# A scheduler that lets instruction packets arrive later, and later still behind queued transfers: the same instructions in another order

## The chip, the cores and the metric

The kernel runs on one core of a Trainium2 chip. The metric is device time in microseconds (us) of one execution; lower is better. Of the core's engines this text names PE (matrix products; its weight loads are a row of their own, PEld), DVE and ACT (elementwise work), POOL, and SP, which here only starts DMA transfers.

## The reference

The input `x` has shape (8, 3200, 256). A filter in the frequency domain comes first, then a gated convolution of what it returns. Cut to what matters:

```python
X = np.fft.rfft(x, axis=1)
Yr = X.real @ w_r - X.imag @ w_i + b_r
Yi = X.real @ w_i + X.imag @ w_r + b_i
Yr, Yi = shrink(Yr), shrink(Yi)          # sign(v) * max(|v| - 0.01, 0)
y = np.fft.irfft(Yr + 1j * Yi, n=3200, axis=1)

gate = sigmoid(sum(conv_w[k] * y_padded[:, k:k + 3200, :] for k in range(5)))
out = (gate * (y @ w_val)) @ w_out
```

## The kernel before, in words

The Fourier transform of length 3200 is split as 64 x 50. Each of the 8 batches goes through two halves.

*Into frequencies.* Eight pieces per batch load `x` and multiply by a 50-point matrix (PE, line 582, tile `p`; line 548 for the first batch). ACT copies the result to `s`, and SP stores it to `a_dram`. From there it comes back transposed as `a`. Thirteen units per batch then do the 64-point step (line 633, `s`), the mixing with `w_r` and `w_i` as three products (line 708 into `k_bank`, line 703 into `y_ps`, lines 666 and 667 for the last unit), bias and threshold on DVE and ACT (`yb`, `tp`), and, for two units at a time, the inverse 64-point step (line 746, `z_ps`; line 738 for the last unit). ACT copies that to `z_t`, SP stores it to `z_dram`.

*Out of frequencies and through the gate.* Eight blocks per batch load `zl` from `z_dram`, which needs the whole batch there, and do the inverse 50-point step (line 802, `y_p`). One `y_p` group is 32 products in the program. The trace shows each product in full fp32 as two weight loads and two matmuls, so the group is 64 weight loads and 64 matmuls of 50 columns. ACT copies it into `y_sb`; ACT and DVE run the five taps and the sigmoid into `acc` (lines 856, 859, 870). PE forms `v_ps` from `y_hl`, DVE multiplies it with the gate (line 901), PE forms `o_ps` from `gated`, and ACT and SP bring `out` home (lines 925 and 927).

*What sets the order.* Nothing here is run in the order in which it is written. `Plan` collects pieces of work with an engine, a duration, their inputs and a due time `at`, and `Plan.order` plays them through on a model of the core. At each step it takes, of the engine that can start first, the piece with the smallest due time among those that can start within some 20 ns. The order so found is the order in which the instructions are issued; on the chip each engine then follows its list strictly and waits on semaphores. The dictionary `O` holds offsets of the due times, one per kind of piece, some for one batch alone, and five other numbers that weigh the choice. They decide the order and nothing else: the pieces, their instructions and their buffers stay the same.

The model also has a rule for PE's instructions. It takes it that PE starts with room for `AHEAD` of them, that a packet of `PACKET` more is asked for each time another `PACKET` have run (the first time after `TRIGGER`), and that a packet can be used `FETCH` ns after it was asked for. A piece of PE whose instructions are not there yet is late in the model, and another may be taken ahead of it. The model's count, `ins`, has matmuls and weight loads in it, not the instructions that only wait on a semaphore. `lines` and `pipe` are the model's times by which the transfers issued so far are done.

Of the kernel before, what the change touches and what calls it, by code (L numbers as in the profile page):

```python
# [83 lines left out]
class Plan:  # L84
# [11 lines left out]
    def add(self, at, engine, busy, fn, uses=(), sets=(), new=None, delay=None, mode="r", kb=0, chain=None, extra=0, moves=1, ways=16, ins=0):  # L96
        n = len(self.pieces)
        before = set()
        for key in uses:
            before |= set(self.writers.get(key, ()))  # L100
        for key in sets:
            before |= set(self.readers.get(key, ())) | set(self.writers.get(key, ()))
        for key in uses:
            self.readers.setdefault(key, []).append(n)
        for key in sets:
            self.writers[key], self.readers[key] = [n], []
        p = dict(n=n, at=round(at, 5), engine=engine, busy=busy, fn=fn, before=before, new=new or {}, mode=mode, kb=kb, extra=extra, moves=moves, ways=ways, ins=ins,
                 tiles={key[:2] for key in (*uses, *sets)}, delay=busy + LAND[engine] if delay is None else delay)
        p["behind"] = {self.last[chain]} if chain in self.last else set()
        if chain:  # L110
            self.last[chain] = n
        self.pieces.append(p)
        return n

    def order(self):
# [25 lines left out]
        mode, pipe = "r", 0.0  # L141
        lines = {10: 0.0, 13: 0.0, 16: 0.0}
        landings = [0.0] * LANES
        ran, fetched = 0, []
        done = []

        def opens(p):
            at = 0.0
            for tag in p["new"].values():
                row = rows[tag]  # L150
                if len(row) >= self.slots[tag]:
                    old = row[len(row) - self.slots[tag]]
                    if users[old]:
                        return None
                    at = max(at, ends[old])
            return at

        while len(done) < len(pieces):
            best = None
            for e in engines:  # L160
                could = []
                for p in waiting[e]:
                    at = opens(p)
                    if at is not None:
                        if p["ins"] and ran + p["ins"] > AHEAD:
                            k = (ran + p["ins"] - AHEAD + PACKET - 1) // PACKET
                            at = max(at, fetched[k - 1] - p["busy"] * max(0, AHEAD + PACKET * (k - 1) - ran) / p["ins"])
                        could.append((max(free[e], p["ready"], at, landings[-LANES] if p["kb"] else 0.0,
                                           max(lines[10], pipe) - BACKLOG if p["kb"] and p["at"] > FIRST else 0.0), p))
                if not could:  # L170
                    continue
                first = min(c[0] for c in could)
                near = [c for c in could if c[0] <= first + SLACK[e]]

                lone = e == "PE" and sum(c[1]["mode"] == "q" for c in near) < O["crowd"]
                if e == "PE" and mode == "q":
                    stay = max(SLACK[e], 100 * min(O["stay"], 4.0))
                    near = [c for c in could if c[0] <= first + (stay if c[1]["mode"] == "q" else SLACK[e])]
                start, p = min(near, key=lambda c: (c[1]["at"] + (0.0 if e != "PE" or c[1]["mode"] != "q" else -O["together"] if mode == "q"
                                                                   else O["hold"] if lone else 0.0), c[0]))  # L180
                if best is None or start < best[0]:
                    best = start, p
            assert best is not None, "no piece can begin"
            start, p = best
            e = p["engine"]
            waiting[e].remove(p)
            busy, delay = p["busy"], p["delay"]
            if e == "PE":
                slow = max([f for until, f in CLOCK if start < until], default=1.0)
                busy, delay = busy * slow, delay * slow  # L190
                to = SWITCH.get(mode + p["mode"], 0)
                busy, delay, mode = busy + to, delay + to, p["mode"]
                while PACKET * len(fetched) + TRIGGER <= ran + p["ins"]:
                    fetched.append(start + p["busy"] * (PACKET * len(fetched) + TRIGGER - ran) / p["ins"] + FETCH)
                ran += p["ins"]
            if p["kb"]:
                ways = p["ways"]
                for n in lines:
                    if n <= ways:
                        lines[n] = max(lines[n], start + LEAD) + p["kb"] * 1024 / ways / RATE  # L200
                pipe = max(pipe, start + LEAD) + p["kb"] * 1024 / PIPE[ways]
                delay = max(pipe, *(lines[n] for n in lines if n <= ways)) + TAIL - start + p["extra"]
                landings += [start + delay] * p["moves"]
            free[e] = start + busy
            end = start + delay
            p["start"], p["end"] = start, end
            done.append(p)
            for t, tag in p["new"].items():
                rows[tag].append(t)
            for t in p["tiles"]:  # L210
                if t in users:
                    users[t] -= 1
                    ends[t] = max(ends[t], end)
            for n, at in [(n, end) for n in after[p["n"]]] + [(n, start) for n in follow[p["n"]]]:
                q = pieces[n]
                q["left"] -= 1
                if q["engine"] == "PE" != e and at == end:
                    at += WEIGHTS
                q["ready"] = max(q["ready"], at)
                if not q["left"]:  # L220
                    waiting[q["engine"]].append(q)
# [15 lines left out]
LEAD, RATE, TAIL = 1080, 20.2, 1270  # L237
PIPE = {10: 235, 13: 300, 16: 324}
LANES = 8
AHEAD, PACKET, TRIGGER, FETCH = 449, 256, 130, 5000  # L240
BACKLOG = 5000
FIRST = -27

# [5 lines left out]
def act(n, kind="copy"):  # L249
# [3 lines left out]

NU = (NT + 1) // 2
T = float(NU)
O = {'stay': -18.479,
     'crowd': -190.568,
     'hold': -218.696,
     'together': 48.138,
     'later': 144.105,  # L260
     'load_x': 172.107,
     'p1': -0.768,
     'p1_step': 1.776,
     'load_a': -165.726,
     's2': -1.563,
     's1i': 3.16,
     'p3': -2.062,
     'load_z': -222.529,
     'y': 23.715,
     'conv': 23.753,  # L270
     'val': 7.511,
     'gate': 9.461,
     'project': 10.677,
     'late_val': 7.079,
     'late_out': 15.503,
     'turn': -157.428,
     'mix_sum': -0.058,
     'p1_1': -93.819,
     'load_x_1': 103.194,
     'p1_2': 16.169,  # L280
     'p3_6': 1.72,
     'p3_7': 2.946,
     'y_7': -11.183,
     'conv_7': 64.044,
     'val_7': 35.136,
     'gate_7': 40.82,
     'project_7': 33.986,
     'p3_1': 0.36,
     'p1_3': -140.856,
     'p3_0': -6.695}  # L290
WARM = 4, 1, 19
SLOTS = {"x": 3, "zl": 3, "y_hl": 2, "s1": 3, "a": 2, "xs": 2, "sx": 2, "xz": 1, "yb": 2, "tp": 3, "zst": 2,
         "acc": 2, "g_hl": 2, "o": 2, "ps_s2": 2, "ps_y": 1, "ps_k": 2, "ps_2": 2, "a_dram": 2, "z_dram": 2}
# [6 lines left out]
def fourier_filter_then_gated_conv(ctx: ExitStack, tc: tile.TileContext, x, w_r, w_i, b_r, b_i,  # L300
# [5 lines left out]
    dram = ctx.enter_context(tc.tile_pool(name="dram", bufs=2, space=bass.MemoryType.DRAM))  # L306
    LATE_VAL, LATE_OUT = set(LATE[int(O["late_val"]):]), set(LATE[int(O["late_out"]):])
    plan = Plan(SLOTS)
# [80 lines left out]
    def from_float64(at, n, views, uses, done, new=None, first=None):  # L389
# [34 lines left out]
        for k, (fn, busy) in enumerate(steps):  # L424
            def piece(k=k, fn=fn):
                if k == 0 and first:
                    first()
                fn()
            add(at + O["later"] + 0.12 * k, "DVE", busy, piece, uses, done, new if k == 0 else None, delay=busy + (130 if k == 12 else 0))

# [599 lines left out]
```

## Time and profile before

| | |
|---|---|
| time, 3 runs | 902.39, 904.09, 911.49 us (median 904.09) |
| the profiled execution | 911.8 us, span 910.0 us |
| PE busy / weight loads | 868.1 us (95%) / 751.2 us (83%), 10,400 each |
| DVE busy | 759.3 us (83%) |
| ACT busy | 603.9 us (66%) |
| mean granted TensorE clock | 0.987 of full speed |
| DMA | 163.34 MB, 179 GB/s |

A busy time is the sum of an engine's instructions. The chain is the work that ended last, followed back from the end step by step to what released it. "Issue" is time in which an engine waited for nothing that the profile shows. The matmuls overlap, so that PE's busy time is not PE at its peak.

### The profile page before, as it was taken

How to read it: one execution, taken by the hardware profiler on the slowest of the kernel's cores; microseconds unless marked ns; L12 is line 12 of the kernel's file. 1: busy time of each engine (PE TensorE's matmuls, PEld its weight loads, DVE VectorE, ACT ScalarE, POOL GpSimd, SP SyncE). 2: the span in 40 equal slices, each digit the busy share in tenths (PEclk: the TensorE clock that was granted, in tenths of full speed). 3: DMA queues.
4: the chain of work that ended last, by engine and by line, in shares of the span. 5: the costliest groups of instructions: out<-in, count | busy, mean ns of one | idle time of the engine just before them, and what ended most of it. 6: DMA issues, size and time to landing. Idle time of an engine off the chain costs nothing.

```text
span 910.0 us, 24569 instructions
## 1 busy us (share of the span) xinstructions
PE 868.1 (95%) x10400; PEld 751.2 (83%) x10400; DVE 759.3 (83%) x1143; ACT 603.9 (66%) x928; POOL 4.4 (0%) x11
## 2 busy tenths in 40 slices
PE   7899999999899998999899999999989999999997
PEld 3678786879789987898789898889879899998775
DVE  2456876999789997799589996899869997999796
ACT  2466646886677667767586767577686766776663
POOL 0000000000000000000000000000001000000000
PEclk9999998999999999999999999999999999999999
DMA  6988885784655467344774577447673546414512
GB/s 217 245 259 252 242 248 175 220 270 158 184 180 168 138 191 230 127 138 141 216 222 139 159 231 215 153 156 209 197 242 99 157 129 195 140 66 146 179 55 91
DMA packets 105289, 163.34 MB, mean 179 GB/s; under 512 B 9690, under 2 KB 78172, under 8 KB 105180
## 3 DMA queue, kind: packets, MB, share of 16 engines
q1 hardware_dynamic: 103764, 158.43, 56.8%
q10 hardware_dynamic: 1416, 3.34, 1.1%
q8 instruction: 82, 1.34, 0.6%
q14 instruction: 27, 0.22, 0.1%
HBM read 82.05 MB, written 79.69 MB: 178 GB/s over the span
## 4 chain that ended last, share of the span: by engine, by line
PE 69%; DVE 18%; DMA 5%; issue 4%; ACT 3%; SPq 0%; ACTq 0%; DVEq 0%
PE y_ps L703 12%; PE o_ps L834 10%; PE v_ps L834 10%; PE s L633 9%; PE z_ps L746 8%; DVE acc L859 7%; PE y_p L802 7%; PE k_bank L708 6%; PE p L582 5%; DMA x<-in_x 3%; DVE acc L901 2%; DVE gated L361 1%; DVE yb L717 1%; DVE yb L714 1%; DVE tp L723 1%
## 5 line engine op out<-in xcount | busy, mean ns | idle before, releaser
L859 DVE SCALAR_TENSOR_TENSOR acc<-y_sb,cw_sb,acc 128x800 f32<-128x800 f32 (+1 forms) x264 | 260.9, 1026 | 9.7 <-ACT acc L856 9.3
L703 PE MATMUL y_ps<-w_sb,xs 128*128 128x256 f32 x1152 | 154.7, 284 | 0.4 <-DVE yb L717 0.2
L834 PE MATMUL o_ps<-gated,wo_sb 128*128 128x400 f32 x756 | 154.8, 354 | 0.0
L703 PEld LDWEIGHTS y_ps<-w_sb,xs 128*128 128x128 f32 x1152 | 143.3, 190 | 6.5 <-issue 1.6
L834 PEld LDWEIGHTS o_ps<-gated,wo_sb 128*128 128x128 f32 x756 | 137.5, 191 | 4.9 <-ACT gated L359 0.8
L834 PE MATMUL v_ps<-y_hl,wv_sb 128*128 128x400 f32 x660 | 130.1, 346 | 0.7 <-DVE acc L901 0.6
L633 PEld LDWEIGHTS s<-f_sb,a 128*128 128x128 f32 x800 | 101.2, 194 | 29.2 <-issue 26.1
L834 PEld LDWEIGHTS v_ps<-y_hl,wv_sb 128*128 128x128 f32 x660 | 118.9, 188 | 2.1 <-DVE acc L901 0.9
L633 PE MATMUL s<-f_sb,a 128*128 128x128 f32 x800 | 114.1, 284 | 2.3 <-ACT sx L683 1.2
L746 PE MATMUL z_ps<-tp,g_sb 64*64 64x256 f32 x1536 | 94.5, 382 | 2.4 <-issue 1.9
L359 ACT CAST gated<-acc 128x800 fp32r<-128x800 f32 x63 | 54.3, 862 | 57.9 <-DVE acc L901 57.7
L708 PE MATMUL k_bank<-w_sb,xs 128*128 128x256 f32 x576 | 90.9, 294 | 1.7 <-ACT xs L687 1.7
L714 DVE TENSOR_TENSOR yb<-k_bank,bias_sb 128x512 f32<-128x512 f32 x96 | 66.1, 688 | 31.3 <-PE k_bank L708 26.4
L802 PE MATMUL y_p<-g_sb,zl 50*64 50x50 f32 x4096 | 74.6, 222 | 16.5 <-issue 15.2
L802 PEld LDWEIGHTS y_p<-g_sb,zl 50*64 50x64 f32 x4096 | 68.1, 136 | 26.7 <-issue 16.9
L721 ACT ACTIVATE tp<-yb,nlam 128x512 f32<-128x512 f32 (+1 forms) x104 | 72.3, 705 | 23.9 <-DVE yb L717 18.4
L708 PEld LDWEIGHTS k_bank<-w_sb,xs 128*128 128x128 f32 x576 | 77.0, 192 | 8.1 <-issue 3.2
L746 PEld LDWEIGHTS z_ps<-tp,g_sb 64*64 64x64 f32 x1536 | 57.9, 134 | 29.1 <-issue 6.7
L717 DVE TENSOR_TENSOR yb<-y_ps,yb 128x512 f32<-128x512 f32 x96 | 66.2, 689 | 15.9 <-PE y_ps L703 15.4
L723 DVE SCALAR_TENSOR_TENSOR tp<-yb,tp 128x512 f32<-128x512 f32 (+1 forms) x104 | 68.0, 670 | 7.9 <-ACT tp L721 7.9
L901 DVE TENSOR_TENSOR acc<-v_ps,acc 128x800 f32<-128x800 f32 x64 | 63.3, 989 | 13.0 <-PE v_ps L834 10.8
L809 ACT COPY y_sb<-y_p 128x800 f32<-128x800 f32 x64 | 52.7, 830 | 26.9 <-PE y_p L802 26.3
(80 smaller groups left out, 1025.5 us busy)
## 6 DMA issues: line engine op xcount, KB each, us to landing
zl<-z_dram SPq DMA_DIRECT2D x128, 200.0 KB
out<-o SPq DMA_DIRECT2D x63, 400.0 KB
a_dram<-s SPq DMA_DIRECT2D x120, 208.0 KB
a<-a_dram SPq DMA_DIRECT2D x96, 256.0 KB
z_dram<-z_t SPq DMA_DIRECT2D x48, 512.0 KB
x<-in_x SPq DMA_DIRECT2D x120, 200.0 KB
a_dram<-s ACTq DMA_DIRECT2D x8, 208.0 KB
x<-in_x ACTq DMA_DIRECT2D x8, 200.0 KB
```

The lines of the kernel that those rows point to most:

```text
L633: nc.tensor.matmul(spec()[:, c, :, i, :], tl[ka][:, i0 + i, c * P:(c + 1) * P], f2_of(i), start=True, stop=True)
L703: nc.tensor.matmul(p[:, 1 - r, :], xm(hx, c, r), w_sb[:, m, hw, c, :], start=k == 0, stop=k == 5)
L708: nc.tensor.matmul(p, sm(hx, c), w_sb[:, 0, hw, c, :], start=k == 0, stop=k == 5)
L714: nc.vector.tensor_tensor(out=buffer(kb, "yb", [P, 2, D]), in0=tl[kk].rearrange("p (a d) -> p a d", a=1).to_broadcast([P, 2, D]), in1=bias ...
L717: add(at + 0.2, "DVE", dve(2 * D), lambda: nc.vector.tensor_tensor(out=yb(), in0=tl[ky], in1=yb(), op=ALU.add), [ky + (0,)], [kb + (0,)])
L721: nc.scalar.activation(out=buffer(kt, "tp", [P, 2, D])[:, 0:n], in_=tl[kb][:, 0:n], func=AF.Relu, bias=nlam)
L723: add(at + 0.2, "DVE", dve(n * D), lambda: nc.vector.scalar_tensor_tensor(out=tl[kt][:, 0:n], in0=tl[kb][:, 0:n], scalar=LAM, in1=tl[kt][: ...
L746: nc.tensor.matmul(p[e * HP:(e + 1) * HP, i, j * D:(j + 1) * D], g[i * HP:(i + 1) * HP, r, e * HP:(e + 1) * HP], tl[kts[j]][i * HP:(i + 1) ...
L802: nc.tensor.matmul(pv[h][e * HP:(e + 1) * HP, c, m, :], zt[half(h), m, c * P + e * HP:c * P + (e + 1) * HP], g2_sb[half(h), :], start=True ...
L834: nc.tensor.matmul(p[:, e, 0:TB], w[:, hw, c, e * P:(e + 1) * P], src(hy, c), start=n == 0, stop=n == 5)
L859: nc.vector.scalar_tensor_tensor(out=acc(c), in0=y_of(c, j), scalar=cw_sb[:, c, j:j + 1], in1=acc(c), op0=ALU.mult, op1=ALU.add)
L901: add(at + own("gate", b), "DVE", dve(2 * TB), lambda: nc.vector.tensor_tensor(out=gate(), in0=hn(tl[kv][:, :, 0:TB]), in1=gate(), op=ALU. ...
```

## The change

Two things change. In `Plan.order`, a packet of PE's instructions is now usable `FETCH` plus 0.6 of the time for which transfers are still queued at the moment it is asked for; `FETCH` goes from 5000 to 5200 ns. And `O` has other numbers: they were chosen anew, by the model's outcome under several such delays. The program's matmuls, elementwise operations and transfers are the same ones; what differs is their order on every engine, and which waits the order needs.

```diff
                 while PACKET * len(fetched) + TRIGGER <= ran + p["ins"]:
-                    fetched.append(start + p["busy"] * (PACKET * len(fetched) + TRIGGER - ran) / p["ins"] + FETCH)
+                    asked = start + p["busy"] * (PACKET * len(fetched) + TRIGGER - ran) / p["ins"]
+                    fetched.append(asked + FETCH + QUEUE * max(0.0, max(lines[10], pipe) - asked))
                 ran += p["ins"]
...
-AHEAD, PACKET, TRIGGER, FETCH = 449, 256, 130, 5000
+AHEAD, PACKET, TRIGGER, FETCH, QUEUE = 449, 256, 130, 5200, 0.6
...
-     'load_z': -222.529,
-     'y': 23.715,
+     'load_z': -29.254,
+     'y': 3.704,
...
```

On PE, before, the first five of the sixth batch's eight `y_p` groups and what stands around them (the same pattern stands in the fourth and fifth batch):

```order
L834 MATMUL v_ps<-y_hl,wv_sb 128x400 x12
L708 MATMUL k_bank<-w_sb,xs 128x256 x6
L802 MATMUL y_p<-g_sb,zl 64x50 x32
L746 MATMUL z_ps<-tp,g_sb 64x256 x16
L802 MATMUL y_p<-g_sb,zl 64x50 x32
L703 MATMUL y_ps<-w_sb,xs 128x256 x12
L802 MATMUL y_p<-g_sb,zl 64x50 x32
L582 MATMUL p_8288<-x,f_sb 64x512 x4
L633 MATMUL s_8298<-f_sb,a 128x2x64 x4
L708 MATMUL k_bank<-w_sb,xs 128x256 x6
L802 MATMUL y_p<-g_sb,zl 64x50 x32
L746 MATMUL z_ps<-tp,g_sb 64x256 x16
```

The same place after the change (lines are one higher):

```order
L835 MATMUL v_ps<-y_hl,wv_sb 128x400 x12
L704 MATMUL y_ps<-w_sb,xs 128x256 x12
L803 MATMUL y_p<-g_sb,zl 64x50 x64
L709 MATMUL k_bank<-w_sb,xs 128x256 x6
L803 MATMUL y_p<-g_sb,zl 64x50 x32
L747 MATMUL z_ps<-tp,g_sb 64x256 x16
L634 MATMUL s_8512<-f_sb,a 128x2x64 x2
L583 MATMUL p_8517<-x,f_sb 64x512 x4
L634 MATMUL s_8512<-f_sb,a 128x2x64 x2
L704 MATMUL y_ps<-w_sb,xs 128x256 x12
L803 MATMUL y_p<-g_sb,zl 64x50 x64
L709 MATMUL k_bank<-w_sb,xs 128x256 x6
```

What moved: the first two `y_p` groups now stand back to back, with a third one six products behind them; the `z_ps` stands behind the three, and the next two groups have a `z_ps`, an `s`, a `p` and a `y_ps` ahead of them. The batch's last `z_ps` stood 9 rows ahead of its first `y_p`; now it stands 32 rows ahead.

On SP, before, the transfers of the same batch from its last store to `z_dram` on:

```order
L764 DMA z_dram<-z_t 128x256
L787 DMA zl<-z_dram 50x1024 x6
L614 DMA a<-a_dram 64x4x256 x2
L927 DMA out<-o 128x2x400
L787 DMA zl<-z_dram 50x1024 x4
L764 DMA z_dram<-z_t 128x4x256
L787 DMA zl<-z_dram 50x1024 x2
L576 DMA x<-in_x 50x1024 x2
L596 DMA a_dram<-s_8301 52x2x512 x2
L787 DMA zl<-z_dram 50x1024 x4
L764 DMA z_dram<-z_t 128x4x256
L576 DMA x<-in_x 50x1024 x2
```

After the change the first six `zl` transfers also follow that store, but eleven rows of other transfers lie between them and the eight rows shown here, which end with the loads for the later blocks:

```order
L597 DMA a_dram<-s_8212 52x2x512 x2
L928 DMA out<-o 128x2x400
L615 DMA a<-a_dram 64x256 x2
L928 DMA out<-o 128x2x400
L788 DMA zl<-z_dram 50x1024 x6
L765 DMA z_dram<-z_t 128x4x256
L597 DMA a_dram<-s_8543 52x2x512 x2
L788 DMA zl<-z_dram 50x1024 x4
```

What moved: before, the store of the batch's last results, all of its `zl` loads and the transfers of the next batches follow each other in one run, and `y_p` begins in the middle of it. Now the first loads come some 20 PE pieces before `y_p` needs them.

## Rows read from the trace of the kernel before

**Rows 1.** The page, busy time of PE (share of the span, instructions).

```profile
PE 868.1 (95%) x10400; PEld 751.2 (83%) x10400; DVE 759.3 (83%) x1143; ACT 603.9 (66%) x928; POOL 4.4 (0%) x11
```

**Rows 2.** The page, the chain that ended last, by engine.

```profile
PE 69%; DVE 18%; DMA 5%; issue 4%; ACT 3%; SPq 0%; ACTq 0%; DVEq 0%
```

**Rows 3.** Waits: engine, line, waited for: us in total, times, longest.

```profile
PEld s L633 <- issue: 26.1, 32, 1.6
...
PE y_p L802 <- issue: 15.2, 8, 3.6
...
PE z_ps L746 <- issue: 1.9, 1, 1.9
...
PE y_p L802 <- DMA zl<-z_dram: 0.8, 2, 0.6
```

**Rows 4.** The page's DMA queues: packets, MB, share of the engines.

```profile
q8 instruction: 82, 1.34, 0.6%
```

**Rows 5.** Windows from the start to four stalls; x counts instructions per engine.

```profile
0.00:247.20 247.20, 232.79 (x2490) 186.09 (x2491) 175.35 (x306) 149.75 (x246) 1.14 (x9) 0.99 0.74 224
...
0.00:359.92 359.92, 342.33 (x4012) 284.52 (x4012) 277.97 (x458) 231.08 (x372) 1.14 (x9) 0.99 0.69 210
0.00:448.20 448.20, 427.42 (x4899) 362.21 (x4900) 358.04 (x575) 290.30 (x463) 1.14 (x9) 0.99 0.66 200
...
0.00:664.40 664.40, 636.88 (x7557) 549.56 (x7557) 544.24 (x849) 443.70 (x693) 1.14 (x9) 0.99 0.65 196
```

**Rows 6.** Timeline of PE in the sixth batch: start, us, instructions, idle before.

```profile
658.28 1.15 PE L802 MATMUL y_p<-g_sb,zl 50*64 50x50 f32 x64
659.25 1.92 PE L746 MATMUL z_ps<-tp,g_sb 64*64 64x256 f32 x32
660.99 1.10 PE L802 MATMUL y_p<-g_sb,zl 50*64 50x50 f32 x64
662.02 1.66 PE L703 MATMUL y_ps<-w_sb,xs 128*128 128x256 f32 x12
663.61 0.79 PE L802 MATMUL y_p<-g_sb,zl 50*64 50x50 f32 x39
666.91 0.60 PE L802 MATMUL y_p<-g_sb,zl 50*64 50x50 f32 x25 [2.50 <-issue]
```

**Rows 7.** Windows: us; PE, PEld, DVE, ACT, POOL; clock, DMA share, GB/s.

```profile
346.70:350.60 3.90, 3.27 (x176) 2.97 (x168) 2.41 (x6) 2.68 (x4) 0.00 (x0) 1.00 0.46 151
356.60:359.92 3.32, 3.32 (x176) 3.02 (x168) 3.32 (x6) 3.32 (x7) 0.00 (x0) 1.00 0.97 248
...
659.04:664.40 5.36, 5.36 (x175) 4.56 (x167) 3.13 (x8) 4.62 (x6) 0.00 (x0) 1.00 0.91 244
672.40:677.50 5.10, 5.10 (x170) 4.41 (x164) 5.10 (x8) 4.68 (x8) 0.00 (x0) 1.00 0.62 209
```

**Rows 8.** Timeline of PE: a wait of 2.93 us in an earlier batch.

```profile
362.85 0.38 PE L802 MATMUL y_p<-g_sb,zl 50*64 50x50 f32 x10 [2.93 <-issue]
```

**Rows 9.** Windows after stalls, and one after a wait for data; clock behind POOL.

```profile
149.00:156.00 7.00, 7.00 (x30) 3.91 (x27) 1.75 (x3) 3.26 (x6) 0.00 (x0) 0.51 0.81 264
364.10:367.50 3.40, 3.40 (x27) 1.79 (x19) 0.11 (x1) 1.93 (x3) 0.00 (x0) 0.50 0.28 114
...
848.80:852.30 3.50, 3.50 (x51) 3.39 (x42) 0.66 (x1) 2.38 (x3) 0.00 (x0) 0.51 0.54 179
```

**Rows 10.** Timeline of PE: two `s` pieces, the second between `y_p` groups.

```profile
226.51 0.61 PE L633 MATMUL s<-f_sb,a 128*128 128x128 f32 x4
226.87 1.64 PE L703 MATMUL y_ps<-w_sb,xs 128*128 128x256 f32 x12
...
244.94 0.71 PE L633 MATMUL s<-f_sb,a 128*128 128x128 f32 x4
245.58 1.15 PE L802 MATMUL y_p<-g_sb,zl 50*64 50x50 f32 x62
```

**Rows 11.** Window near the end, when no `y_p` is left.

```profile
875.00:900.00 25.00, 23.96 (x100) 17.85 (x98) 23.96 (x32) 13.05 (x19) 0.00 (x0) 1.00 0.20 75
```

More of the change, by code (lines that the diff above doesn't have):

```diff
@@ L255 @@
 T = float(NU)
[L256 to L267, printed above, removed]
-     'load_z': -222.529,
-     'y': 23.715,
[L270 to L273, printed above, removed]
+O = {'stay': -42.085,
+     'crowd': -50.453,
+     'hold': 7.335,
+     'together': 155.775,
+     'later': 18.484,
+     'load_x': 192.178,
+     'p1': -1.787,
+     'p1_step': 1.293,
+     'load_a': -41.005,
+     's2': -2.447,
+     's1i': 2.145,
+     'p3': 2.825,
+     'load_z': -29.254,
+     'y': 3.704,
+     'conv': 5.188,
+     'val': 5.514,
+     'gate': -19.992,
+     'project': 8.565,
      'late_val': 7.079,
      'late_out': 15.503,
[L276 to L290, printed above, removed]
+     'turn': -153.706,
+     'mix_sum': -0.971,
+     'p1_1': -89.715,
+     'load_x_1': 85.875,
+     'p1_2': 25.498,
+     'p3_6': -1.759,
+     'p3_7': -0.606,
+     'y_7': 18.885,
+     'conv_7': -29.176,
+     'val_7': 13.441,
+     'gate_7': -17.01,
+     'project_7': 13.598,
+     'p3_1': -0.93,
+     'p1_3': -6.723,
+     'p3_0': 0.056}
 WARM = 4, 1, 19
```

## The prediction

> **What bounds the kernel now.** I read the chain first: PE has 69% of it and DVE 18% [rows 2], and PE is busy for 95% of the span [rows 1]. So the end is set by how densely PE's list runs, up to the last batch's `y_p`. In the last 35 us or so DVE takes over: 23.96 of 25 us busy there [rows 11]. Since the instructions stay the same, only PE's gaps and its slow stretches can change before that point. Next I read the waits. PE hardly waits for data: 0.8 us for `zl` [rows 3]. What it waits for is "issue", 15.2 us at `y_p` in 8 places and 1.9 us at `z_ps` in one, 17.1 us in all.
>
> What these waits are can be counted. Up to four of them PE has run 4,981, 8,024, 9,799 and 15,114 matmuls and weight loads [rows 5]. The steps are 3,043, 1,775 and 5,315; that is 12, 7 and 21 times 256, less 29, 17 and 61. About 1% is missing each time, which fits instructions that only wait and are not in the count. PE stops at the same place in every packet of 256. And there is a queue of its own for instructions, with 82 packets and 1.34 MB [rows 4], 16 KB each; 82 times 256 is PE's whole list. So PE has run dry of instructions. It happens among the `y_p` groups because these use them up fastest: 128 in about 1.0 us, against 64 in 1.74 us for `z_ps` and 24 in 1.6 us for `y_ps` [rows 6].
>
> How long a packet takes is seen in pairs. Each stretch of [rows 7] begins some 320 instructions ahead of a packet's end (449 less 130, the scheduler's own constants) and ends there or just behind; PE runs about 340 in each. From 659.04 it runs 5.36 us of work and then waits 2.50 us more [rows 6, 7]. From 672.40 the same sequence of pieces, the next in the list, takes 5.10 us, without a wait. The DMA engines were busy for 0.91 of the first and 0.62 of the second. Likewise 3.90 us were enough at a share of 0.46, while 3.32 us of work at 0.97 were followed by 2.93 us of waiting [rows 7, 8]. So a packet needs 4 to 5 us where transfers are thin and 6 to 8 us where they are dense.
>
> A second loss follows the longer waits. From 364.10 on, just after the wait of 2.93 us, the granted clock is 0.50 for 3.4 us, which is 1.2 instead of 2.4 GHz; after the wait of the last batch it is 0.51 for 3.5 us [rows 9]. There are five such stretches, each costing half its length, 1.7 us, so 8.6 us. A sixth, of 7 us, begins at 149 [rows 9], a hundred us ahead of the first stall of [rows 5]; the change does not aim at it.
>
> **The change, part by part.**
>
> *The rule on packets* alone issues nothing and costs nothing.
>
> *The waits for instructions.* I laid the durations of [rows 6] over both orders and cut both lists where PE's packets end, waiting instructions included. The result is a count of places, an estimate. Before, 13 of 81 packets leave less than 5.5 us of work between the request, 319 instructions ahead, and the last instruction at hand; 3 of them leave less than 3.6 us. After the change there are 10, but 6 of them leave less than 3.6: those of the two adjoining groups with a third close behind. So there are fewer tight places, and deeper ones. In their favour stands the order on SP: before, `y_p` starts in the middle of the run of a `z_dram` store, six `zl` loads, `a`, `x` and `a_dram`; after, its first loads lie far ahead, and what is started in the 5 us before a tight place in the middle batches is an `a`, an `out` or a `zl`. With thin transfers I take 4.5 us for a packet, the middle of the quick rows. The six deep places (3.5 us of work on average, two of them in the last batch about 1 us less) then wait 1 us each in the middle and 2 us each at the end, 8 us; the other four and what is left in the looser ones, 1 us. Together 9 us instead of 17.1, a gain of 8. Bounds: at the shortest time that a row shows to be enough, 3.9 us [rows 7], 4 us are left (0.4 in four places, 1.4 in two), a gain of 13; 10 places times the 2.93 us of the dense row is 29 us, a loss of 12.
>
> *The clock.* The waits after which it fell are the longer ones of the row, those around 2 us and more. With 1 us in the middle batches I leave two, in the startup or the last batch: three fewer, a gain of 5 us. The ends are the full 8.6 us and a loss of about the same, if each batch gets one more.
>
> *More alternation.* PE's groups of small-array pieces (`p`, `z_ps`, `y_p`) are interrupted by full-array ones 90 times instead of 84. A half `s` piece takes 0.36 us among its like and 0.64 us between two `y_p` groups [rows 10], so 0.28 us per interruption, 6 times: 1.7 us lost. The weight loads idle longer there, 0.8 us in each of 32 [rows 3], but the matmuls in flight cover most of that; 0.8 would make it 5 us.
>
> *Room between stages.* Between an `s` and the `y_ps` that uses it there is now about twice the PE work (an estimate, the same durations laid over both orders), and `zl` loads start earlier before use. As PE waited for such data hardly at all [rows 3], I put this at 0, with 3 us as the most to win. What it risks is that more pieces in flight share the same buffers; a wait for one would show on PE.
>
> *The last batch.* Its `y_p` groups still come about 11 us of PE work behind its last `z_ps`, and DVE's run of taps after it has the same pieces. I put it at 0.
>
> The sum against the profiled execution: 911.8 - 8 - 5 + 1.7 = 900.5 us. That execution is 7.7 us above the median of the runs shown, 904.09. Nothing else in the trace varies so easily as the time a packet takes, so I hold that the median execution lost about 18 of the 25.7 us (17.1 + 8.6) instead. In the same proportion (12.4 of 25.7 remain) the changed kernel would lose 8.7 there: 904.1 - 9.3 + 1.7 = 896.5. I predict between the two, **898 us**.
>
> **Rivals.**
>
> *No fewer waits: 905 us.* The scheduler counts without the waiting instructions; by the fourth batch its packets lie over a hundred instructions beside PE's. By its own count the new order has one tight place; by PE's count it has ten. If depth and number balance, and the transfers make no difference, the loss stays and the 1.7 us are added: 904.1 + 1.7, about 905, within 901 to 910. For it speaks that the count of places falls by 3 only; against it the twin stretches, where transfers alone decided. The Trainium skill's page "Runtime: NRT & Kernel Launch", section "Instruction fetch mechanics", would lead here too: it gives PE room for 2,048 instructions and calls the refill in blocks of 256 mostly hidden. By that, the waits would have another cause and the estimate would be 904.1 + 1.7, too. The trace agrees on the blocks of 256 [rows 4, 5] and not on the hiding.
>
> *One deep wait in each batch: slower, 919 us.* Where the packet's end falls among the `y_p`, `y_p`, `k_bank`, `y_p` of a batch, some 3.5 us of work stand against 6 to 8 us if transfers are dense after all, since each finished `y_p` frees a buffer and starts a `zl` load at once. That would be a wait of 3.5 us and 1.7 us of half clock in six batches, 31 us, against the 18 lost in the median execution: 904.1 + 13 + 1.7, about 919, within 911 to 923. It decides from a mean wait of about 2.5 us per batch on. Against it: less stands in the queues at these places than before.
>
> *The waits nearly vanish: 888 us.* If packets come in 3.5 us in the middle batches, a little quicker than the quick rows, only the last batch waits, 3 us, the clock does not fall, and the room between stages brings its 3 us: 904.1 - 18 + 3 + 1.7 - 3, about 888, within 884 to 892.
>
> **How the numbers follow.** My forecast (between 890 and 903) has a chance of 0.52, no fewer waits 0.24, the slower case 0.12, the waits gone 0.12. A measurement of this kernel tells about 1% from no change, 9 us here; its own three runs lie 9 us apart. Faster than 895 is the last case and just under half of the forecast, 0.36 together; slower than 913 is most of the slower case, with a little of the second, 0.11; between them 0.53. The range of 8 in 10 leaves out the better half of the best case and most of the slower one: 887 to 910.
>
> **What would show it.** In the changed profile the "issue" waits of `y_p` and `z_ps` should add up to 6 to 12 us, the longest of them in the first two batches or the last, and stretches at half clock should be two or three besides the one near 149 us. The sum of PE's other waits should not grow. The forecast is wrong if "issue" stays at 17 us or more, if a wait for `a`, `zl` or `x` appears on PE in the middle batches, or if the time from the last batch's first `y_p` to the end changes by more than 3 us.

## The result, and the profile after

The changed kernel takes **880.42 us** (median of 4 runs, 878.76 to 881.72) against 905.51 for the kernel before, measured beside it (4 runs, 902.39 to 911.49): a ratio of 0.9714, 95% interval 0.9658 to 0.9771. It is faster by 2.9%. The forecast of 898 us had the direction; its range, 887 to 910, does not hold the time.

The profiled execution took 881.6 us, its span is 879.8. The page of the changed kernel, busy times, then the instruction queue, then the chain by engine:

```profile
PE 857.8 (97%) x10400; PEld 745.5 (85%) x10400; DVE 759.1 (86%) x1143; ACT 604.9 (69%) x928; POOL 3.8 (0%) x11
...
q8 instruction: 82, 1.34, 0.6%
...
PE 78%; DVE 15%; DMA 3%; ACT 2%; issue 1%; SPq 0%; ACTq 0%; DVEq 0%
```

The same instructions in the same 82 packets [rows 1, 4]; on the chain PE rose from 69% to 78% and "issue" fell from 4% to 1% [rows 2]. PE's waits after the change (us in total, times, longest), and the weight loads' wait that [rows 3] begin with:

```profile
PE z_ps L739 <- DVE acc L902: 2.9, 1, 2.9
PE y_p L803 <- issue: 2.2, 5, 1.0
...
PEld s L634 <- issue: 19.0, 26, 0.8
```

Of 17.1 us of waits for instructions [rows 3] 2.2 are left. A window over one batch, from its last `z_ps` to the next batch's, shows what that does in the middle. The columns are those of [rows 7]. Before:

```profile
540.00:646.60 106.60, 103.44 (x1291) 92.48 (x1290) 92.80 (x137) 75.59 (x114) 0.00 (x0) 0.98 0.62 188
```

After, the same batch:

```profile
508.90:610.70 101.80, 101.73 (x1293) 91.22 (x1292) 92.57 (x137) 75.33 (x116) 0.00 (x0) 1.00 0.63 196
```

PE now works through the whole batch, 101.73 of 101.80 us at full clock; before, it stood still for 3.2 us and lost the rest to a clock of 0.98. The timeline of the changed kernel at the deep place of that stretch shows no wait in it at all, where the prediction took 1 us (start, us, instructions, in brackets the idle time before):

```profile
551.84 2.08 PE L803 MATMUL y_p<-g_sb,zl 50*64 50x50 f32 x128
553.86 0.97 PE L709 MATMUL k_bank<-w_sb,xs 128*128 128x256 f32 x6
554.76 1.42 PE L803 MATMUL y_p<-g_sb,zl 50*64 50x50 f32 x61
```

**The account.** The names below the difference are those of the experiments. For every run I took three sums from the trace: PE's idle time right where a packet of its list begins (the 450th instruction, then every 256th, those that only wait counted in), half the length of the stretches at a granted clock of about 0.5, and the rest of the span. The first is a little more than the "issue" waits listed, since short waits count too.

| profiled execution | span | idle at packets | half of the half-clock time | rest |
|---|---|---|---|---|
| before | 910.0 | 18.8 | 11.9 | 879.3 |
| changed | 879.8 | 2.2 | 5.5 | 872.1 |
| difference | 30.2 | 16.6 | 6.4 | 7.2 |
| numbers_only | 882.8 | 2.7 | 8.5 | 871.6 |
| rule_only | 914.3 | 15.0 | 10.2 | 889.1 |
| b_shift128 | 899.2 | 14.8 | 5.1 | 879.4 |
| a_shift112 | 880.0 | 3.7 | 1.7 | 874.6 |
| a_traffic | 895.2 | 4.1 | 14.3 | 876.9 |
| a_dense | 880.8 | 5.8 | 0.7 | 874.3 |
| b_thin_out | 908.1 | 14.5 | 18.7 | 874.9 |
| b_p3 | 919.6 | 5.0 | 17.0 | 897.6 |
| a_p3 | 923.3 | 4.1 | 22.1 | 897.0 |
| b_start | 913.6 | 13.5 | 23.1 | 877.1 |
| a_start | 889.7 | 5.3 | 3.6 | 880.9 |
| a_conv6 | 894.8 | 0.7 | 15.9 | 878.1 |

More than half of the gain is the waits for instructions, a fifth the clock, a quarter something else. The last two can't be parted sharply. Between kernels with PE's order the same, the rest differs by up to 2.5 us (changed, a_shift112, a_dense), and the changed kernel has the lowest of the three. It was charged 3.4 us for two half-clock stretches in its first 60 us; a_dense, with the same order there and no such stretch, has run the same 900 matmuls 2.3 us earlier (121.0 against 123.3 us). By a_dense's rest the third part would be 5.0 us in place of 7.2. The execution of before that was profiled is one of its slower ones: between the medians the difference is 25.1 us.

### The profile page after: what moved, and what is told of

The parts are those of the page before. It is cut to its first block, busy times and chain, and to the rows that moved or that the text cites. A ratio compares the mean times of both kernels' runs of the same rounds, so it can differ in the third digit from the quotient of the medians.

```text
span 879.8 us, 24544 instructions
## 1 busy us (share of the span) xinstructions
PE 857.8 (97%) x10400; PEld 745.5 (85%) x10400; DVE 759.1 (86%) x1143; ACT 604.9 (69%) x928; POOL 3.8 (0%) x11
## 4 chain that ended last, share of the span: by engine, by line
PE 78%; DVE 15%; DMA 3%; ACT 2%; issue 1%; SPq 0%; ACTq 0%; DVEq 0%
PE y_ps L704 14%; PE o_ps L835 12%; PE v_ps L835 11%; PE s L634 9%; PE z_ps L747 8%; PE k_bank L709 7%; PE y_p L803 6%; DVE acc L860 6%; PE p L583 5%; DMA x<-in_x 2%; PE warm L951 1%; DVE acc L902 1%; PE v_ps L831 1%; DMA f_sb<-in_f 1%; DVE gated L362 1%
## 5 line engine op out<-in xcount | busy, mean ns | idle before, releaser
L704 PE MATMUL y_ps<-w_sb,xs 128*128 128x256 f32 x1152 | 157.7, 286 | 0.7 <-DVE yb L718 0.7
L835 PEld LDWEIGHTS o_ps<-gated,wo_sb 128*128 128x128 f32 x756 | 135.6, 189 | 3.4 <-issue 1.0
L634 PE MATMUL s<-f_sb,a 128*128 128x128 f32 x800 | 111.9, 280 | 1.3 <-DVE xs L692 1.2
L688 ACT CAST xs<-s 128x512 fp32r<-128x512 f32 x96 | 56.2, 586 | 43.0 <-PE y_ps L704 28.1
L709 PE MATMUL k_bank<-w_sb,xs 128*128 128x256 f32 x576 | 85.3, 283 | 0.4 <-DVE yb L715 0.4
L709 PEld LDWEIGHTS k_bank<-w_sb,xs 128*128 128x128 f32 x576 | 74.8, 188 | 5.1 <-issue 1.1
L926 ACT COPY o<-o_ps 128x800 f32<-128x800 f32 x63 | 51.9, 823 | 38.0 <-PE o_ps L835 37.8
L803 PEld LDWEIGHTS y_p<-g_sb,zl 50*64 50x64 f32 x4096 | 66.1, 135 | 13.9 <-issue 5.1
L803 PE MATMUL y_p<-g_sb,zl 50*64 50x50 f32 x4096 | 71.8, 220 | 3.4 <-issue 2.2
```

The source lines that it names most:

```text
L634: nc.tensor.matmul(spec()[:, c, :, i, :], tl[ka][:, i0 + i, c * P:(c + 1) * P], f2_of(i), start=True, stop=True)
L688: nc.scalar.copy(out=tl[kx][:, 0:512], in_=tl[k2].rearrange("p a b -> p (a b)"))
L704: nc.tensor.matmul(p[:, 1 - r, :], xm(hx, c, r), w_sb[:, m, hw, c, :], start=k == 0, stop=k == 5)
L709: nc.tensor.matmul(p, sm(hx, c), w_sb[:, 0, hw, c, :], start=k == 0, stop=k == 5)
L803: nc.tensor.matmul(pv[h][e * HP:(e + 1) * HP, c, m, :], zt[half(h), m, c * P + e * HP:c * P + (e + 1) * HP], g2_sb[half(h), :], start=True ...
L835: nc.tensor.matmul(p[:, e, 0:TB], w[:, hw, c, e * P:(e + 1) * P], src(hy, c), start=n == 0, stop=n == 5)
```

## The experiments

**Which half of the change carries it: *numbers_only* (new numbers, old rule) and *rule_only* (new rule, old numbers).**

```diff
 numbers_only:
-    fetched.append(asked + FETCH + QUEUE * max(0.0, max(lines[10], pipe) - asked))
+    fetched.append(start + ... + FETCH)        # FETCH = 5000; O as in the change
 rule_only: the same lines the other way round, O as before
```

> The new numbers with the old rule: the other part alone. The PE list differs from that of the changed kernel in a few places. If the numbers carry the gain: issue waits under 6 us, ratio 0.970 to 0.980. If the rule does: 12 us of waits and more, ratio 0.99 to 1.01.

> The new rule on packets with the old numbers: one part of the change alone. If the rule itself steers y_p clear of dense transfers, issue waits fall to under 8 us and the time to 885 to 895 (ratio 0.978 to 0.989). If the numbers carry the gain, since they alone move y_p away from the run of transfers behind the z_dram store, issue waits stay at 12 us or more and the ratio is 0.99 to 1.01.

Numbers alone: ratio 0.9736 (0.9693 to 0.9779), which can't be told from the whole change. Rule alone: 1.011 (1.0069 to 1.0151), slower. PE's waits of rule_only:

```profile
PE y_p L803 <- issue: 15.0, 11, 3.5
PE k_bank L709 <- ACT xs L688: 1.7, 2, 1.0
```

So the rule by itself did not bring the gain. With the old numbers it only moves the places about: 15.0 us of idle time at packets stay, and the rest rises to 889.1 us.

**Does the place where a packet ends matter, with the order untouched: *b_shift128* and *a_shift112*.** In b_shift128, 32 tiny products (128 instructions) follow the first warm-up, so that every later packet of the kernel before ends 128 instructions earlier in the same order; a_shift112 does the same to the changed kernel with 28.

```diff
+        for j in range(32):
+            nc.tensor.matmul(pw[e * HP:(e + 1) * HP, ...], tl[ki][half(h), 0:HP], tl[ki][half(h), 0:N2], ...)
```

> The kernel before with 32 tiny products more behind the first warm-up products (128 weight loads and matmuls on the tile of zeros, some 2 us, in a stretch where PE waits for x). Every other instruction and the order are the same; only the places at which PE's packets of 256 end move by half a packet along the list. Laid out with the durations of the trace, the places with less than 5.5 us of work ahead of a packet's end fall from 13 to about 4. Theory A (the change won its time by taking away waits for packets, and the half clock after them): the issue waits of y_p and z_ps fall from 17.1 to 3 to 7 us, the half-clock stretches after them from five to one or two, and the time by 12 to 20 us, ratio to the kernel before 0.978 to 0.988. Theory B (the gain came from the longer way between a stage and the next that uses it, for data): nothing of that is touched, so the time stays or rises by the 2 us, ratio 1.000 to 1.003.

> The changed kernel with 28 such tiny products (112 instructions) at the same place: same order, packets end elsewhere; tight places under 5.5 us fall from 10 to about 3. Theory A: the 2.2 us of issue waits left and the extra microseconds around them go, 1 to 3 us less than the changed kernel in spite of the 2 us of filler, ratio to the kernel before 0.968 to 0.972. Theory B: 0 to 2 us more than the changed kernel, ratio 0.971 to 0.974.

b_shift128: 0.993 (0.9899 to 0.996). Its waits on PE:

```profile
PE y_p L802 <- issue: 8.0, 6, 3.7
PE z_ps L746 <- issue: 2.5, 1, 2.5
```

The rest of the span is that of the kernel before to 0.1 us, so the gain came from packets and clock alone, which is Theory A's account. Neither theory had the size: only 4 us fewer at packets, since transfers are as dense as before, and late packets at the new places took 4.8 to 9.2 us from the request to the first instruction. a_shift112 came out at 0.9706 (0.967 to 0.9742), the same as the changed kernel. That is inside Theory A's range, but not by its mechanism: "issue" rose from 2.2 to 3.7 us instead of going. It tells nothing apart.

**Are packets late because of transfers: *a_traffic*, *a_dense*, *b_thin_out*.** a_traffic adds two transfers of 200 KB at each `zl` load of the changed kernel:

```diff
+            for j in range(2):
+                spare = dram.tile([P, 4 * D], F32, name="spare", tag="spare", bufs=8)
+                nc.sync.dma_start(out=spare[half(j % 2), :], in_=more[...])
```

> The changed kernel with one more transfer beside every load of zl: the same bytes again, from x into a scratch tensor in DRAM that nobody reads (64 blocks, 2 x 200 KB each). PE's, DVE's and ACT's orders are those of the changed kernel, packets end at the same instructions. It makes the transfers around y_p dense again. If thin transfers are what lets packets come in time (theory A): the issue waits of y_p and z_ps rise from 2.2 to 8 us or more, a packet that ends in y_p, y_p, k_bank, y_p takes over 5 us, the clock falls to half after some of them, and the time rises by 8 to 25 us over the changed kernel (ratio to before 0.98 to 1.00). If the order on PE alone did it (packets are in time because PE uses them up later), issue waits stay under 4 us and the time rises by less than 5 us, by waits for zl, a or x if at all.

0.986 (0.9817 to 0.9903), slower than the changed kernel by 13 us, though not for the reason expected. By the table most of it is half clock (14.3 us in place of 5.5) and the rest of the span (876.9 in place of 872.1):

```profile
PE y_p L807 <- DMA zl<-z_dram: 4.3, 7, 0.9
PE p L583 <- DMA x<-in_x: 3.4, 1, 3.4
...
PE y_p L807 <- issue: 2.7, 3, 2.2
```

Theory A had named 8 us of "issue" and got 2.7. The trace tells why: at two deep places of the middle batches (457.8 and 559.1 us) the added transfers started after the packet had been asked for, and the packets still took 3.6 and 3.8 us. Two packets that did meet them landed late, after 6.5 instead of 3.5 us and after 7.2 instead of 3.3. So I put the transfers ahead of the request. a_dense issues four of them in the batches 3 to 6, right behind the load of the last `a`:

```diff
+            for j in range(4 if last and 3 <= b <= 6 else 0):
+                spare = dram.tile([P, 4 * D], F32, name="spare", tag="spare", bufs=8)
+                nc.sync.dma_start(out=spare[half(j % 2), :], in_=more[...])
```

> The changed kernel with four more transfers of 200 KB (x to a scratch buffer in device memory, no part of the result) issued in each of the batches 3 to 6 right behind the load of the batch's last `a`, some 4 us ahead of the packet requests at the deep places; PE's order is unchanged. Theory A (a packet's time is set by what is queued on the DMA engines when it is asked for; the changed kernel is quick because at its deep places nothing is): the packets 39, 49 and 70, usable 3.6 to 3.8 us after the request in the changed kernel, take 5 us or more there; PE waits 1.5 to 3 us at two to four of these places and is at half clock for 3.4 us behind each; issue waits 5 to 10 us in all, time 889 to 897 (ratio to the kernel before 0.982 to 0.991). Theory B (the packets' time has little to do with transfers; the places alone count): issue waits stay under 3 us and the time within 3 us of the changed kernel's 880. If PE waits for `a`, `zl` or `x` instead, it says nothing of either.

Two windows of the changed kernel, from the request to the first instruction of the packet, with the DMA share as the last number but one:

```profile
450.51:454.27 3.76, 3.53 (x176) 3.22 (x168) 3.70 (x9) 3.26 (x6) 0.00 (x0) 1.00 0.39 117
...
653.00:657.59 4.59, 4.17 (x161) 3.72 (x159) 4.13 (x9) 4.06 (x6) 0.00 (x0) 1.00 0.36 104
```

The same two and a third in a_dense:

```profile
448.58:453.41 4.83, 3.53 (x175) 3.22 (x168) 4.32 (x9) 3.27 (x6) 0.00 (x0) 1.00 0.75 210
551.29:555.01 3.72, 3.53 (x177) 3.21 (x169) 3.67 (x9) 3.55 (x6) 0.00 (x0) 1.00 0.73 220
653.45:659.31 5.86, 4.14 (x161) 3.69 (x160) 5.10 (x10) 4.07 (x6) 0.00 (x0) 1.00 0.68 199
```

And its timeline behind the first of them (the wait is in brackets):

```profile
450.97 1.14 PE L807 MATMUL y_p<-g_sb,zl 50*64 50x50 f32 x61
453.41 0.26 PE L807 MATMUL y_p<-g_sb,zl 50*64 50x50 f32 x2 [1.30 <-issue]
...
657.04 0.55 PE L807 MATMUL y_p<-g_sb,zl 50*64 50x50 f32 x20
659.31 0.84 PE L807 MATMUL y_p<-g_sb,zl 50*64 50x50 f32 x43 [1.72 <-issue]
```

PE does the same 3.53 and 4.1 us of work in the first and the third of these windows, in the same order; with the transfers in front the packet needs 4.83 and 5.86 us, and PE waits. In the second window the packet was not late (3.72 us; 3.60 in the changed kernel), though the extra transfers stood in front of it as well: from the request to the start of the packet's own transfer the DMA engines were busy for other queues at a share of 0.59, against 0.71 and 0.65 in the other two. Why this one was quick stays open. Of the three packets that the expectation named, 39 is the first window and 49 the second; no extra transfers stood ahead of 70 (756.6 us), which took 3.4 us, and the third window is packet 59. "Issue" rises from 2.2 to 5.0 us, the low end of what Theory A gave, and no stretch at half clock follows these waits. The time, 0.9756 (0.971 to 0.9803), is below the 0.982 that Theory A gave; it lies some 4 us above the changed kernel's, within the intervals of both, so it can't be told from it; the waits can.

b_thin_out takes transfers away from the kernel before instead (most of `out` is not written):

```diff
-    nc.sync.dma_start(out=dst, in_=tl[ko])
+    nc.sync.dma_start(out=dst[0:32, 0:1], in_=tl[ko][0:32, 0:1])
```

> The kernel before, with the stores of out cut from 400 KB to 51 KB each (32 of 128 partitions, one of two halves: most of out isn't written), same order, same places of the packets; some 22 of 163 MB less. Theory A: with less in the queues packets come sooner, issue waits fall from 17 to 8 to 13 us and the time by 5 to 12 us (ratio 0.987 to 0.995). If the stores of out don't stand where the packets are asked for, nothing moves (ratio 0.997 to 1.000). Theory B (data): no change of issue waits; any gain appears as fewer waits for data.

0.9911 (0.9879 to 0.9942): inside the range of Theory A, but not by the waits that it named, as far as the trace tells: 14.3 us of "issue" at `y_p` remain in the profiled execution. That one is the slowest of its ten (899.51 to 909.88 us), so what the quicker ones saved stays open, and so does whether the `out` stores stand in front of late packets.

**Is it the distance of the blocks from the data: *b_p3* and *a_p3*.** One number, p3, moves the blocks of the middle batches as a whole, by 4.9 units. b_p3 gives the kernel before the changed one's, a_p3 the reverse.

```diff
 b_p3:                        a_p3:
-     'p3': -2.062,          -     'p3': 2.825,
+     'p3': 2.825,           +     'p3': -2.062,
-     'p3_7': 2.946,         -     'p3_7': -0.606,
+     'p3_7': -1.941,        +     'p3_7': 4.28,
```

> The kernel before with one number of the changed kernel: the due time of the blocks behind the frequencies (y_p and what follows), 4.9 units later for the batches in the middle, the last batch's kept. y_p then stands over 30 us of PE work behind its batch's last z_ps, as in the changed kernel. If this distance is the ingredient that thins the transfers at y_p: issue waits fall to under 8 us, ratio 0.975 to 0.988. If the other numbers are needed too: 12 us and more, ratio 0.99 to 1.01.

> The opposite: the changed kernel with the blocks due 4.9 units earlier in the middle batches, as before. y_p stands again close behind the z_dram store. If the distance is the ingredient: issue waits rise to 10 us or more, ratio 0.985 to 1.00. If not: under 6 us, ratio 0.97 to 0.98.

Both are slower than the kernel before: 1.0099 (1.0073 to 1.0125) and 1.0146 (1.0127 to 1.0166). In b_p3 the idle time at packets fell from 18.8 to 5.0 us, which the move was to bring; but PE then waited for data, and the rest rose from 879 to 898:

```profile
PE s L633 <- DMA a<-a_dram: 3.9, 1, 3.9
PE o_ps L834 <- ACT o L925: 3.8, 3, 1.6
PE y_p L802 <- DVE acc L901: 3.3, 1, 3.3
PE z_ps L746 <- ACT y_sb L809: 2.9, 3, 2.4
```

In a_p3 "issue" hardly grew, to 3.2 us, and data waits cost the time:

```profile
PE y_ps L704 <- DVE yb L718: 6.3, 5, 2.2
PE y_p L803 <- DVE acc L902: 5.7, 3, 4.6
PE y_p L803 <- DMA zl<-z_dram: 5.3, 3, 4.3
```

Each expectation held in half: in b_p3 the waits fell as if the distance were the ingredient, in a_p3 they stayed low as if it were not, and neither time followed. So a number that brings the blocks away from late packets is only worth something together with the others that keep the data ahead.

**Where the rest of the gain lies: *b_start* and *a_start*.** Six numbers apply to the batches 0 to 3 alone. b_start gives the new six to the kernel before, a_start the old six to the changed one.

```diff
 b_start (a_start is the reverse, in the changed kernel):
-    'p1_1': -93.819, 'load_x_1': 103.194, 'p1_2': 16.169, 'p3_1': 0.36, 'p1_3': -140.856, 'p3_0': -6.695
+    'p1_1': -89.715, 'load_x_1': 85.875, 'p1_2': 25.498, 'p3_1': -0.93, 'p1_3': -6.723, 'p3_0': 0.056
```

> The kernel before with the six new numbers that apply to the batches 0 to 3 alone (p1_1, load_x_1, p1_2, p1_3, p3_0, p3_1), old rule. The order is the old one up to the 130th and from the 361st of PE's 724 rows on, so only about 100 to 420 us can differ. Theory A (about 4 us of what is unexplained lies in the order of the first batches): the time outside of packet waits and half clock falls by 3 to 5 us from 879, most of it before 250 us; with fewer tight packets in that stretch (one of under 4 us of work in place of three) some 4 to 7 us of waits and half clock go too; 893 to 899 in all (ratio 0.984 to 0.992). Theory B (it came with the numbers for all batches): only the waits change, 898 to 902 (0.990 to 0.996), the rest stays at 879.

> The changed kernel with those six numbers of the kernel before put back. Its first batches then differ from both kernels; from about 440 us on it is the changed kernel. Theory A: the time outside of packet waits and half clock rises by 3 to 5 us from 872, the packet places stay much the same (two more of 3.5 us of work): 883 to 888 (ratio 0.975 to 0.981). Theory B: 879 to 883 (0.971 to 0.975).

b_start is the same as before: 1.0005 (0.9973 to 1.0036). Idle time at packets fell to 13.5 us and the rest by 2.2, to 877.1, but its profiled execution was 46.1 us at half clock instead of 23.8, and it is the slowest of its ten. a_start: 0.9819 (0.9777 to 0.986), about 9 us above the changed kernel, just beyond Theory A's 0.981; the rest of the span rose by 8.8 us, about twice the 3 to 5 that Theory A gave. I marked in each trace the moment by which PE has done the same 250 us of its work (its pieces weighed by their durations). From 122 us, where the kernels are about level (a_start some 1.5 us ahead), the changed kernel gets there in

```profile
122.00:288.00 166.00, 163.94 (x2231) 142.93 (x2230) 154.30 (x239) 122.91 (x191) 0.00 (x0) 1.00 0.65 201
```

The kernel before:

```profile
122.00:294.90 172.90, 167.57 (x2258) 144.36 (x2257) 151.97 (x233) 124.03 (x189) 0.00 (x0) 0.98 0.63 195
```

And a_start:

```profile
122.00:293.90 171.90, 165.85 (x2222) 143.59 (x2222) 151.05 (x235) 122.24 (x187) 0.00 (x0) 0.99 0.64 195
```

With the old six numbers back, the changed kernel loses in these batches as the kernel before did: PE idles for 6.0 us instead of 2.1 (before: 5.3) at a clock of 0.99 instead of 1.00 (before: 0.98). From 400 us of work on its distance to the changed kernel stays at 9.7 to 10.3 us. So some 7 of the 30 us are gained in the first batches (2.2 of them at packets, 3.4 of clock in the kernel before), and the six numbers bring them only beside the others.

**A version to beat both: *a_conv6*.** It moves the taps of the seventh batch back, to spare the last `z_ps` its 2.9 us.

```diff
+     'conv_6': 6,
```

> A version meant to beat both: the changed kernel with the due time of the seventh batch's taps 6 units later, so that DVE takes the product with `v_ps` ahead of the taps around the last `z_ps`. Theory A (the 2.9 us that the last `z_ps` waits for DVE, and the 3.4 us at half clock behind it, are lost on PE's path): both go, 2 to 4.6 us gained, 876 to 878. Theory B (DVE has the same work left and is the bound from there on): the wait comes back later at `v_ps` or `o_ps` of the last batch, 879 to 883.

0.9871 (0.9829 to 0.9912): slower than the changed kernel by 14 us, far beyond Theory B's end. The wait of `z_ps` is gone; PE waits for DVE further on instead,

```profile
PE y_p L803 <- DVE acc L902: 4.6, 2, 3.3
PE o_ps L835 <- DVE acc L902: 4.5, 2, 3.8
```

and is at half clock for 13.7 us from 842.4 us on, where the 3.3 us wait of `y_p` ends. No version here is better than the change; a_shift112 and numbers_only are level with it.

## Why the prediction was wrong, point by point

**What bounds the kernel** held. PE's list runs dry of instructions, and that is where most of the gain came from. The missing 1% was the semaphore waits and the like in PE's list: with these 241 instructions counted in, every wait of PE for "issue" in the kernel before comes after 449 plus a multiple of 256 instructions, to within one. Nothing in the sums of other work changed (DVE 759.3 and 759.1 us).

**The step that failed: how long a packet takes at the deep places.** The prediction counted ten tight places, six of them deep, and the changed kernel has them. It then took "thin" transfers for them, rightly, and 4.5 us for a packet there, "the middle of the quick rows". Measured in the records of the instruction queue, from the request to the first instruction of the packet: 3.8, 3.6 and 3.8 us at three deep places (450.5, 552.1 and 754.8 us), hardly more than PE's work there, so that it waits 0.1 to 0.2 us instead of 1 us each. The window of the first stands above; those of the other two:

```profile
552.07:555.67 3.60, 3.53 (x175) 3.21 (x168) 3.60 (x8) 3.52 (x6) 0.00 (x0) 1.00 0.31 91
...
754.84:758.60 3.76, 3.57 (x164) 3.25 (x163) 2.49 (x4) 3.46 (x6) 0.00 (x0) 1.00 0.50 144
```

Between the request and the start of the packet's own transfer the DMA engines did nothing for other queues at two of these places (share 0.00) and were busy for them at 0.62 at the third. The transfer began 1.1 to 1.4 us after the request, had landed after 2.3 to 2.6, and the first instruction ran 1.2 to 1.4 us behind that. In the kernel before, at eight of the ten places where PE idled over 0.5 us, the transfer began 3.7 to 8.6 us after the request, at shares of 0.7 to 1.0 until then. The two quick rows of [rows 7] could not be averaged. In the row of 3.90 us PE idled the last 0.67 us until the packet came, so 3.90 is what that packet took. In the row of 5.10 us PE did not wait: the packet had landed 2.7 us after the request, and 5.10 is only PE's work. In the last batch the packets took 4.6 and 3.7 us, and PE waited 1.0 and 0.3 us instead of 2 each. In all 2.2 us against the 9 that the prediction left; the bound of 4 us at "the shortest time that a row shows to be enough" was nearly right.

The change did not make packets quick in general. The transfer of 32 of its 81 packets begins over 3 us after the request, against 34 of 81 before; but before, PE ran dry at 8 of these, and after the change at none, since the late ones fall where PE has enough work at hand.

That transfers in front can make a packet late is shown by a_dense: same order, same places, four transfers put in front, and two of the three packets behind them became 1.1 and 1.3 us slower. The third did not, so transfers in front do not decide alone. The fourteen traces together say the same, for all packets asked for after 120 us: where other queues kept the DMA engines under 5% busy in the first microsecond after the request, the packet's transfer began 1.8 us after it (median of 208, 0.8 to 8.9); where they kept them over 90% busy, 3.2 us (226, 1.1 to 7.2). b_shift128 is the reverse of a_dense: other places, same transfers, 14.8 us at packets. The Trainium skill, page "Runtime: NRT & Kernel Launch", section "Instruction fetch mechanics", calls the refill mostly hidden: by the trace that holds for the changed kernel (2.2 us for 82 packets) and not for the kernel before (17.1 us of the same 82).

**The clock.** The prediction left two stretches of 3.4 us of the five behind waits for instructions; in the changed kernel none of the five is left. Four others cost 5.5 us. One lies behind the `z_ps` that waits for DVE,

```profile
803.80:807.20 3.40, 3.03 (x9) 2.88 (x10) 3.40 (x5) 1.23 (x2) 0.00 (x0) 0.50 0.55 193
```

two lie in the first 60 us, and one at the very end. The gain is 6.4 us, not 5; the stretch near 149 us, which the prediction said the change does not aim at, went too. The order there is another; that this is the cause was not tried.

**Alternation** was priced at 1.7 us and can't be seen: between 250 and 700 us of PE's work the loss outside of packets and half clock grew by 14.3 us before and 12.2 after, and the waits of the weight loads of `s` fell from 26.1 to 19.0 us instead of rising.

**Room between stages** was put at 0, with 3 us as the most. The rest of the span fell by 7.2 us (5.0 by a_dense's, see the account): 4.7 by 250 us of PE's work, 2.1 between 250 and 700, the remainder behind. The prediction looked at waits for data in sum over the whole trace and for `zl`, `a` and `x`; it passed over 1.6 us of `p` for ACT's `y_sb` and 1.7 of `k_bank` for `xs` in the first two batches, neither of which is in the list after the change. a_start, whose rest is 8.8 us higher, shows that it is the order there. How the 7.2 us split among single waits stays open: PE's gaps of over 0.15 us outside of packets add up to 18.2 us before and 15.3 after, 2.9 less.

**The last batch** took 66.0 us from its first `y_p` to the end before and 62.2 after, 3.8 less; the prediction had put it at 0 and said that more than 3 would speak against it:

```profile
844.00:910.00 66.00, 58.12 (x704) 44.79 (x704) 49.98 (x62) 36.28 (x48) 0.00 (x0) 0.97 0.31 105
...
817.60:879.80 62.20, 55.83 (x705) 43.41 (x704) 50.12 (x62) 36.30 (x48) 0.00 (x0) 0.99 0.32 111
```

The waits for instructions there are 0.6 us less, half clock 1.3, and PE waits some 0.8 us less for ACT and DVE; the last microsecond I could not place.

**The rule alone** was said to cost nothing. With the old numbers it costs 1.1%; with the new ones it makes no difference that can be measured.

**The range.** The rival that came true is "the waits nearly vanish", 888 us, to which the prediction gave 0.12; the measured 880.42 lies below even its 884 to 892. Its own time was 8 us too high, because it kept 3 us of waits in the last batch (1.3 measured) and 1.7 for alternation, and gave the room 3 instead of 7. The sum against the profiled execution, 900.5, stands against 881.6: 6.8 us of waits (2.2 left in the place of 9), 1.4 of clock, 1.7 of alternation and 7.2 of room make 17 of the 19 us; the rest are waits too short for the list. Drawing the sum towards the median brought the forecast 2.5 us nearer to the measured time, which was luck: the reason given, packets that vary between executions, was not tested.

## What to carry to other kernels

When an engine waits for "issue" at equal distances in its list, the price of a packet is not a constant: measure it from the request to the first instruction, and look at what stands in the DMA queues when it is asked for. Lay the dense run of small instructions where few transfers are queued; the count of tight places alone said little here (13 before and 10 after, 17.1 and 2.2 us of waits). A scheduler's parts are not additive: single parts of the change put into the kernel before (b_p3, b_start, rule_only) were worth nothing or cost 1%, and one number of the changed kernel set back (a_p3) cost more than the whole gain.

## What the runs showed of the hardware that was not expected

The same wait is not always followed by half clock. In three kernels the last `z_ps` waits 2.93 or 2.94 us for DVE. In the changed kernel 3.4 us at a granted clock of 0.50 follow (above), in numbers_only 6.8 us:

```profile
801.90:808.70 6.80, 6.16 (x18) 5.96 (x19) 6.21 (x7) 2.06 (x3) 0.00 (x0) 0.50 0.28 96
```

In a_dense none:

```profile
805.30:808.70 3.40, 2.80 (x15) 2.78 (x16) 3.40 (x5) 1.19 (x2) 0.00 (x0) 1.00 0.55 193
```

In the kernel before 3.4 us follow a wait of 2.1 us at 572 us:

```profile
572.30:575.70 3.40, 3.40 (x14) 3.38 (x13) 2.33 (x4) 2.50 (x5) 0.00 (x0) 0.50 0.75 227
```

In b_start, with the same pieces there, 6.8 us go with one of 2.2 at 567 us:

```profile
566.90:573.70 6.80, 6.46 (x29) 4.82 (x29) 3.39 (x6) 4.09 (x6) 0.00 (x0) 0.50 0.50 160
```

And the changed kernel has two stretches of 3.4 us in its first 60 us, where a_dense, with the same list up to 348 us, has none. This may be much of why runs of the kernel before lie 10 us apart (903.41 to 913.37 in 13 runs) and those of the changed one 3 (4 runs). That was not tried by itself.
